# Two products of no use ahead of each transposition, and a transposition whose PSUM banks hold halves of the heads

## The chip, the core and the metric

The kernel runs on one core of a Trainium2 chip. A core has a matrix engine (TensorE, in profiles PE; its weight loads are shown as PEld), VectorE (DVE), ScalarE (ACT), GpSimd (POOL) and SyncE (SP), each with its own in-order queue of instructions; DMA engines move data. They wait for one another by semaphores. TensorE writes to PSUM, in banks, and ScalarE and VectorE read them there. The metric is the device time of one execution in microseconds (us); lower is better.

## What is computed

A block-sparse attention (4 batches, 8 heads, 768 positions, 64 per head, blocks of 32), and behind it a mixing of tokens and channels:

```python
    mask = np.abs(blk_i - blk_j) <= window
    mask = mask | (blk_i == 0) | (blk_j == 0) | (blk_i == n_blocks - 1) | (blk_j == n_blocks - 1)
    for qb in range(n_blocks):
        for kb in sampled_blocks[qb]:
            mask[qb * block:(qb + 1) * block, kb * block:(kb + 1) * block] = True
    ...
    attn = np.exp(scores)
    attn = attn / (np.sum(attn, axis=-1, keepdims=True) + 1e-09)
    return np.matmul(attn, v).astype(np.float32)
...
    theta = x @ w_theta
    ...
    y = yr + yi
    u = x + y
    return (u + np.maximum(u @ w_ch, 0.0)).astype(np.float32)
```

Each block of 32 queries sees its neighbours, the first and last block and three blocks drawn at random; the first and the last block see all. The change concerns the attention alone, in f32.

## The kernel before, in words

The attention is cut into 56 units (lines 441 to 443): for each of two pairs of batches, six *outer* units (marked "w": the first and last query block against a third of all keys each) and 22 *inner* ones, one for each query block between. An inner unit holds one query block of 16 heads: two batches b, four places p (these lie on the partitions, 4 x 32 queries) and two halves e of the heads, against 8 key blocks (256 keys). All units pass these stages:

- `scores` (line 320): TensorE writes S, per (e, b) 128 queries by 256 keys, two banks of PSUM; VectorE reduces it to the extreme m (line 342).
- `weights` (line 352): ScalarE makes P = exp, four instructions, one for each (e, b), in the order e0b0, e0b1, e1b0, e1b1 (line 359).
- `turn` (line 363): TensorE transposes P with the help of the identity, eight times 128x128, into T, two PSUM banks of four each (line 369). Bank 0 holds the first 128 keys of all four (e, b), bank 1 the others. The four transpositions into bank 0 come first. The pool for T has two buffers, both used by each unit, so a unit's bank h is free when `evict` of the unit before has read its bank h.
- `evict` (line 371): ScalarE copies the two banks to pT in SBUF, one instruction each (line 375).
- `values` (line 378): TensorE multiplies pT with the values: `va` holds the first 128 keys' rows (window and edge blocks), `vb` the others (gathered); the sum over both is made in PSUM as X (line 393), 64 records in the profile for an inner unit.
- `finish` (line 404): VectorE divides X by the sum of its weights (lines 400 to 402); `store` writes it out.

The order is written out by hand (`manual_schedule`, line 462). The loop at line 490 puts, for step n, into the queues: the scores of unit n+1, gathering of keys for n+3 (GpSimd), a share of an unrelated job for VectorE and ScalarE (decoding the weights of the token mix, class `Decoder`), `turn` of n, `values` of n-1, `evict` of n, `weights` of n+1, a key copy and the scaling of queries for n+3 on ScalarE, `finish` of n-1, loads for later units. So TensorE's queue runs S(n+1), T(n), X(n-1), S(n+2), T(n+1), ..., and ScalarE's P(n), key copy, scaling, decoding, eviction(n), P(n+1).

Ahead of all units, TensorE makes ten products of the identity with itself that nothing reads (lines 470 to 472). Behind the units, the token mix (from line 548) runs to the end. In the profile, names with `_w` are the outer units': `T_w`, `P_w`.

Of the kernel before, what the change touches and what calls it, by code (L numbers as in the profile page):

```python
# [183 lines left out]
def attention(tc, qT, qE, kT, vr, sampled, xs, ident, early_pieces, late_pieces, first_places, follow, spares):  # L184
# [13 lines left out]
    nc = tc.nc  # L198
    with ExitStack() as ctx, ExitStack() as early:
# [60 lines left out]
        def number_blocks(bp, i):  # L260
            def load(k0, k1, engine):
                _, values = nc.values_load_multi_w_load_instructions(
                    tab.block[0:1, 3 * i + k0 : 3 * i + k1], engines=[engine], min_val=0, max_val=NB - 1,
                    skip_runtime_bounds_check_because="Tables clamps the block numbers",
                )
                return list(values)

            numbers[bp, i] = load(0, 2, mybir.EngineType.Pool) + load(2, 3, mybir.EngineType.Activation)
# [94 lines left out]
        def turn(unit):  # L363

            s = st[unit]
            pt = s.pop("P")
            s["T"] = banks = [ps_t.tile([P, 4, 128], F32, tag="T", name=f"T{name(unit)}_{h}") for h in range(2)]
            for k in range(8):
                nc.tensor.transpose(banks[k // 4][:, k % 4], pt[:, (k // 2) % 2, k % 2, 128 * (k // 4) : 128 * (k // 4) + 128], ident)  # L369

        def evict(unit):
            s = st[unit]
# [5 lines left out]
        def values(unit):  # L378
            bp, i, x = unit
            s = st[unit]  # L380
            s["X"] = ps_x.tile([P, 2, 2, 65], F32, tag="X", name=f"X{name(unit)}")
            if i == "w":
                t, a = x
                parts, width = [(wide[bp][2 * t + c], 128) for c in range(2)], 64
            else:
                parts = [(vas[i % 2], 96 if i == 1 else 128), (vbs[(i + 1) % VB], 96 if i == NB - 2 else 128)]
                a, width = 0, 32
            for b in range(2):
                for e in range(2):
                    for c, (v, rows) in enumerate(parts):  # L390
                        for w_ in range(128 // width):
                            rr, v0 = slice(width * w_, width * w_ + width), 260 * (2 * b + e) + 65 * (2 * a + w_)
                            nc.tensor.matmul(  # L393
                                s["X"][rr, b, e, :], s["T"][0:rows, 4 * c + 2 * e + b, rr], v[0:rows, v0 : v0 + 65], start=c == 0, stop=c == 1,
                            )

        def normalised(label, x, out):
# [48 lines left out]
        def name(unit):  # L446
            bp, i, x = unit
            return f"{bp}_w{x[0]}{x[1]}" if i == "w" else f"{bp}_{i}"
# [13 lines left out]
        with tc.manual_schedule():  # L462
# [27 lines left out]
            for n in range(steps):  # L490
# [16 lines left out]
                if due > 1 and decoder.at % 3:  # L507
                    decoder.on_vector()
                do(n, turn)
                do(n - 1, values)  # L510
                if len(units) - 2 <= n < len(units):
                    next(follow)
# [434 lines left out]
```

## Time and profile before

| | |
|---|---|
| three runs | 593.34, 595.84, 599.29 us (median 595.84) |
| profiled execution, its own time | 595.23 us |
| its span, first to last instruction | 593.5 us |
| mean granted TensorE clock | 0.976 of full speed |
| attention part | up to about 252 us of the span |
| token mix | from there to the end |

The profile is a record of one execution: a page with busy times, groups of instructions by source line and a chain of waits from the last instruction back, and views of single stretches in order of time. In a row of a group, `T<-ident,P 128*128 128x128` is what is written and read (weights 128x128 f32), `x352` the number of records, then busy us and mean ns of one, then the idle us of the engine in front of them and who ended it. An f32 product shows as two records with a weight load each, a transposition as one. In a row of a stretch stand the start in us, the length, the engine, the line and operation, the number merged into the row, and in brackets the idle time ahead and what ended it. "issue" is idle time in which the engine waited for nothing that the profile shows. PEclk is the clock granted to TensorE.

### The profile page before, as it was taken

What the parts mean: (1) busy time and instruction counts of PE and PEld (TensorE: products, weight loads), DVE (VectorE), ACT (ScalarE), POOL (GpSimd) and SP (SyncE); (2) the same over time, 40 slices, a digit from 0 to 9 for tenths busy, and PEclk for the clock granted to TensorE, in tenths of its full rate; (3) what the DMA queues carried; (4) which work ended last, traced back from release to release, by engine and by line L of the source; (5) the groups of instructions that cost most, each with busy time, mean ns of one, the idle gap of its engine ahead of it and who ended that gap; (6) DMA issues with size and microseconds to landing.
All of it is one profiled execution on the core that took longest, in us unless ns stands there. A gap on an engine that the chain in (4) does not pass through costs nothing.

```text
span 593.5 us, 17325 instructions
## 1 busy us (share of the span) xinstructions
PE 547.3 (92%) x7092; PEld 434.5 (73%) x7092; DVE 426.5 (72%) x846; ACT 335.3 (57%) x684; POOL 185.6 (31%) x281
## 2 busy tenths in 40 slices
PE   6997786779988888899999999999999999999997
PEld 4775554556645655688888888888888888888886
DVE  3778998978799989879999995657722659614252
ACT  4798687768967878766474562345530446421220
POOL 1389869922588899520000000000000000000000
PEclk9899989889998989999999999999999999999999
DMA  8979999879987988842333132310202311102002
GB/s 311 351 222 270 263 264 253 251 207 313 273 229 211 260 240 225 227 128 76 85 110 87 36 94 86 104 53 8 83 20 80 99 36 35 36 27 81 1 1 106
DMA packets 53087, 86.67 MB, mean 146 GB/s; under 512 B 5392, under 2 KB 31632, under 8 KB 52624
## 3 DMA queue, kind: packets, MB, share of 16 engines
q1 hardware_dynamic: 43200, 53.28, 29.0%
q0 software_dynamic: 6944, 22.85, 14.3%
q10 hardware_dynamic: 2864, 9.44, 5.2%
q8 instruction: 56, 0.92, 0.7%
q14 instruction: 23, 0.19, 0.1%
HBM read 72.95 MB, written 12.58 MB: 144 GB/s over the span
## 4 chain that ended last, share of the span: by engine, by line
PE 73%; DVE 14%; DMA 6%; issue 3%; ACT 2%; SPq 0%; DVEq 0%; ACTq 0%
PE ya L668 23%; PE yb L668 11%; PE T L369 5%; PE S L339 4%; DVE m L342 4%; PE h L609 4%; PE X L393 4%; PE h L612 4%; PE h L610 4%; PE o L693 3%; PE o L694 3%; PE o L695 2%; PE X_w L393 2%; PE T_w L369 2%; DMA k<-in_kT_dram 2%
## 5 line engine op out<-in xcount | busy, mean ns | idle before, releaser
L359 ACT ACTIVATE P<-S,m 128x256 f32<-128x256 f32 x176 | 70.0, 498 | 15.1 <-DVE m L342 13.9
L369 PE MATMUL T<-ident,P 128*128 128x128 f32 x352 | 61.3, 299 | 16.0 <-ACT P L359 12.6
L369 PEld LDWEIGHTS T<-ident,P 128*128 128x128 f32 x352 | 41.2, 146 | 44.7 <-ACT P L359 35.5
L342 DVE TENSOR_REDUCE m<-S 128x4 f32<-128x1024 f32 x44 | 53.5, 1216 | 9.2 <-PE S L339 7.5
L339 PE MATMUL S<-kg,q 64*32 64x256 f32 x1408 | 54.2, 395 | 5.7 <-issue 5.4
L668 PE MATMUL ya<-w_values,zh 128*128 128x512 f32 x160 | 59.4, 395 | 0.0
L375 ACT COPY pT<-T 128x512 f32<-128x512 f32 x88 | 47.8, 599 | 12.9 <-PE T L369 12.6
L393 PE MATMUL X<-vb,pT 128*32 128x65 f32 (+1 forms) x1408 | 48.2, 227 | 6.9 <-issue 6.9
L393 PE MATMUL X<-va,pT 128*32 128x65 f32 (+1 forms) x1408 | 48.8, 230 | 6.1 <-issue 5.5
L313 POOL DMA_INDIRECT vb<-in_vr_dram,rows x44 | 44.5, 1012 | 19.5 <-PE X_w L393 9.2
L297 POOL COPY kg<-k 128x256 f32<-128x256 f32 (+2 forms) x66 | 37.5, 585 | 33.0 <-DMA k<-in_kT_dram 15.9
L668 PE MATMUL ya<-w_keys,zh 128*128 128x512 f32 x128 | 47.6, 396 | 0.0
L276 POOL COPY kg<-k 128x256 f32 x88 | 46.3, 552 | 0.0
L701 DVE SCALAR_TENSOR_TENSOR of<-o,xT 128x512 f32<-128x512 f32 (+1 forms) x24 | 13.3, 557 | 45.7 <-PE o L695 42.5
L393 PEld LDWEIGHTS X<-va,pT 128*32 128x32 f32 (+1 forms) x1408 | 34.1, 114 | 14.7 <-issue 12.2
L668 PE MATMUL yb<-w_values,zh 128*128 128x256 f32 x160 | 44.6, 278 | 0.0
L393 PEld LDWEIGHTS X<-vb,pT 128*32 128x32 f32 (+1 forms) x1408 | 36.2, 115 | 8.7 <-issue 8.6
L306 POOL COPY va<-va 32x1040 f32<-32x1040 f32 (+1 forms) x28 | 32.5, 1160 | 23.3 <-DMA va<-in_vr_dram 13.6
L609 PE MATMUL h<-w_theta_hi,xh 128*128 128x512 f32 x96 | 38.2, 398 | 0.4 <-ACT xh L598 0.4
L625 DVE SCALAR_TENSOR_TENSOR rr<-t,h 128x512 f32<-128x512 f32 x24 | 16.5, 687 | 29.8 <-ACT t L619 29.8
L610 PE MATMUL h<-w_theta_lo,xh 128*128 128x512 f32 x96 | 37.9, 395 | 0.0
L339 PEld LDWEIGHTS S<-kg,q 64*32 64x32 f32 x1408 | 22.8, 108 | 19.1 <-issue 10.3
(175 smaller groups left out, 1460.0 us busy)
## 6 DMA issues: line engine op xcount, KB each, us to landing
va<-in_vr_dram SPq DMA_DIRECT2D x58, 130.0 KB
q<-in_qT_dram SPq DMA_DIRECT2D x22, 256.0 KB
xs<-xo SPq DMA_DIRECT2D x22, 256.0 KB
xr<-xs SPq DMA_DIRECT2D x22, 256.0 KB
xa<-xs SPq DMA_DIRECT2D x88, 64.0 KB
raw_tok_r<-in_w_tok_r_dram ACTq DMA_DIRECT2D x8, 576.0 KB
out_dram<-of SPq DMA_DIRECT2D x16, 256.0 KB
v<-in_vr_dram SPq DMA_DIRECT2D x6, 520.0 KB
```

The source lines that it names most:

```text
L276: nc.gpsimd.tensor_copy(*sampled_keys(bp, i, k))
L297: nc.gpsimd.tensor_copy(kgs[i % 2][:, s0 : s0 + n], ks[bp][:, b0 : b0 + n])
L313: nc.gpsimd.indirect_dma_start(out=vbs[(i + 1) % VB][rows], out_offset=None, in_=vr, in_offset=bass.IndirectOffsetOnAxis(ap=tab.rows[rows, ...
L339: nc.tensor.matmul(sc[32 * p : 32 * p + 32, e, b, :], q[rows, b, p, :], keys[rows, :, 4 * b + p, :], start=True, stop=True)
L342: nc.vector.tensor_reduce(m.rearrange("r (e b) -> r e b", e=2), sc, axis=AX.X, op=ALU.min)
L359: nc.scalar.activation(pt[:, e, b], sc[:, e, b], AF.Exp, bias=m[:, 2 * e + b : 2 * e + b + 1], scale=-1.0)
L369: nc.tensor.transpose(banks[k // 4][:, k % 4], pt[:, (k // 2) % 2, k % 2, 128 * (k // 4) : 128 * (k // 4) + 128], ident)
L375: nc.scalar.copy(out[:, 4 * h : 4 * h + 4], bank)
L393: nc.tensor.matmul(s["X"][rr, b, e, :], s["T"][0:rows, 4 * c + 2 * e + b, rr], v[0:rows, v0 : v0 + 65], start=c == 0, stop=c == 1,)
L609: nc.tensor.matmul(ps, hi[:, c, :], wh[:, c, :], start=c == 0, stop=False)
L610: nc.tensor.matmul(ps, hi[:, c, :], wl[:, c, :], start=False, stop=False)
L668: nc.tensor.matmul(acc, z[:, dd], wt[:, t0 : t0 + n], start=first and (n == 512 or c % 2 == 0), stop=last, skip_group_check=n == 256,)
```

## The change

Ahead of each inner unit's transposition, TensorE multiplies the identity by itself twice, once into the last quarter of each of the two banks of T, where a transposition afterwards writes over it; no one reads the two products. For inner and outer units alike, bank e now holds the four transposed quarters of head half e (both batches b, both key halves c) where bank c held key half c; the eight transpositions come in the order e, b, c. `values` goes through (e, b) where it went through (b, e), and reads the quarters from their new places. `evict` is the same code.

```diff
             s["T"] = banks = [ps_t.tile([P, 4, 128], F32, tag="T", name=f"T{name(unit)}_{h}") for h in range(2)]
-            for k in range(8):
-                nc.tensor.transpose(banks[k // 4][:, k % 4], pt[:, (k // 2) % 2, k % 2, 128 * (k // 4) : 128 * (k // 4) + 128], ident)
+
+            for h in range(2 if unit[1] != "w" else 0):
+                nc.tensor.matmul(banks[h][:, 3], ident, ident, start=True, stop=True)
+            for e in range(2):
+                for b in range(2):
+                    for c in range(2):
+                        nc.tensor.transpose(banks[e][:, 2 * b + c], pt[:, e, b, 128 * c : 128 * c + 128], ident)
...
-            for b in range(2):
-                for e in range(2):
+            for e in range(2):
+                for b in range(2):
                     for c, (v, rows) in enumerate(parts):
...
-                                s["X"][rr, b, e, :], s["T"][0:rows, 4 * c + 2 * e + b, rr], v[0:rows, v0 : v0 + 65], start=c == 0, stop=c == 1,
+                                s["X"][rr, b, e, :], s["T"][0:rows, 4 * e + 2 * b + c, rr], v[0:rows, v0 : v0 + 65], start=c == 0, stop=c == 1,
```

## The prediction

> **What bounds the kernel now.** I read the page first, then the busy time of the attention part alone, then the groups of instructions, then the chain of waits. The edit touches only the attention part, from about 28 to 252 us; the token mix behind it is left as it is.
>
> ```profile
> span 593.5 us, 17325 instructions
> core 0: us, PE busy (x) PEld busy (x) DVE busy (x) ACT busy (x) POOL busy (x), PEclk, DMA share, GB/s
> 28.00:252.00 224.00, 187.86 (x4916) 128.67 (x4916) 194.97 (x340) 176.99 (x414) 167.52 (x238) 0.95 0.87 247
> ```
>
> No engine fills these 224 us: VectorE is busy for 195 (87%), TensorE for 188 (84%), ScalarE for 177 (79%). The order of work is a ring, so what matters is who waits in each step. TensorE does in step n the scores of unit n+1, the transposition T of unit n and the values X of unit n-1; T needs ScalarE's four exponentials P, and ScalarE's eviction of T stands ahead of its next exponentials.
>
> ```profile
> L369 PE MATMUL T<-ident,P 128*128 128x128 f32 x352 | 61.3, 299 | 16.0 <-ACT P L359 12.6 <-ACT q L246 1.2 <-ACT kg L279 0.5
> L375 ACT COPY pT<-T 128x512 f32<-128x512 f32 x88 | 47.8, 599 | 12.9 <-PE T L369 12.6
> ```
>
> So the ring stalls both ways: TensorE sat idle 16.0 us in front of transpositions, 12.6 of it for P, and ScalarE 12.9 us in front of evictions, 12.6 of it for T. Which of the two holds in a unit is seen from the weight loads of its transposition. Two units side by side, then the first and last of each kind:
>
> ```profile
> 50.04 1.58 ACT L359 ACTIVATE P<-S,m 128x256 f32<-128x256 f32 x4
> 52.12 0.85 PEld L369 LDWEIGHTS T<-ident,P 128*128 128x128 f32 x8 [0.41 <-ACT kg L279]
> 52.81 1.08 ACT L375 COPY pT<-T 128x512 f32<-128x512 f32 x2 [0.89 <-PE T L369]
> ...
> 207.83 1.57 ACT L359 ACTIVATE P<-S,m 128x256 f32<-128x256 f32 x4 [1.41 <-DVE m L342]
> 208.36 0.14 PEld L369 LDWEIGHTS T<-ident,P 128*128 128x128 f32 x1 [1.03 <-ACT P L359]
> 209.45 0.53 PEld L369 LDWEIGHTS T<-ident,P 128*128 128x128 f32 x5 [0.23 <-ACT P L359]
> ...
> 33.03 1.09 PE L369 MATMUL T<-ident,P 128*128 128x128 f32 x8
> 250.47 1.02 PEld L369 LDWEIGHTS T<-ident,P 128*128 128x128 f32 x8
> ...
> 66.25 0.14 PEld L369 LDWEIGHTS T<-ident,P 128*128 128x128 f32 x1 [1.70 <-ACT P L359]
> 244.96 0.14 PEld L369 LDWEIGHTS T<-ident,P 128*128 128x128 f32 x1 [0.71 <-ACT P L359]
> ```
>
> At 52.12 P had long been written (50.04 + 1.58): TensorE comes late, all eight go in a row, and ScalarE waits 0.89 us for them. At 208.36 P is late: the first transposition waits 1.03 us, the next ones go one for each exponential, and the fourth P releases five at once. Of the 44 inner units 26 are of the first kind (33.03 to 250.47), 13 of the second (66.25 to 244.96), and 5 lie between (they start behind the scores but still wait for the last P).
>
> **The price of a product of no use.** Nothing in the inner units is an f32 product of two 128x128 operands. The nearest row is the warm-up of the same two operands, ten products at the start:
>
> ```profile
> L472 PE MATMUL idle<-ident x20: 274/421/583, 1.7 to 5.8; 128*128 128x128 f32 x20
> L369 PE MATMUL T<-ident,P x352: 269/273/477, 33.0 to 251.5; 128*128 128x128 f32 x176
> 33.10 1.02 PE T L369 x8
> ```
>
> Ten products are 20 records, so one product is two. They start 0.216 us apart ((5.8 - 1.7) / 19). But their durations (min 274, median 421) lie as those of T do between its median at full clock (273) and its longest (477): most of the warm-up ran at half clock. Halved, a record is 0.108 us. From the other side, T's records, one weight load and one pass of 128 columns each, go at 1.02 / 8 = 0.128 us. Four records for two products are therefore 0.43 to 0.51 us; 0.86 if the warm-up's pace were that of the full clock. I take 0.51, by the row of the same place in the program. 44 units make 22 us of new TensorE time, some of it in front of the transposition's own work.
>
> **Its wait.** The first product into each bank now carries the wait for unit n-1's eviction of that bank; behind it in TensorE's queue stand T, X and the next scores. That eviction (52.81 + 1.08 = 53.89 in the example) stands before P of the unit on ScalarE, so it is over before P is; I cost this wait at nothing. The cover is P itself.
>
> **A late TensorE pays all.** In the 26 units the products stand between the scores and the transposition, and nothing waits there: T ends 0.51 us later, 1.02 where the clock is halved. The new order gives nothing back: the first bank is still whole after four of eight.
>
> **A late P gains.** In the 13 units the products run in the idle time (1.03 us at 208.36 against 0.51). After the last P only two transpositions are left, not five: 3 x 0.128 = 0.38 us off the end of T, X and the next scores. In the 5 between, the two meet: the later of "scores + 0.51 + 1.02" and "last P + two transpositions" decides; worked out, 0.43, 0.29 and 0.22 later, 0.13 and 0.19 earlier. The 12 outer units only get the order. X's four groups only change places with the same 64 records, and their evictions were made a step before: nothing.
>
> Over all units this would be 26 x 0.51 - 13 x 0.38 + 0.62 = +8.9 us. But only the transpositions on the chain of waits count:
>
> ```profile
> 60.65 1.02 PE T L369 x8
> 156.67 1.03 PE T L369 x8
> 219.01 1.88 PE T L369 x8
> ...
> 77.03 1.04 PE T L369 x5
> 174.58 0.77 PE T L369 x5
> 246.06 0.77 PE T L369 x5
> ...
> 78.07 1.89 PE X L393 x64
> 79.96 1.43 PE S L339 x32
> 55.26 1.67 issue
> 90.52 2.38 issue
> 96.62 1.86 issue
> ```
>
> On it are ten late-TensorE units at full clock (33.10 to 156.67): 10 x 0.51 = 5.1; the one at 219.01 at half clock: 1.0; two of the units between: 0.7. Together +6.8 us. Against this four late-P units (77.03, 174.58, one at 209.46, 246.06): 4 x 0.38 = 1.5; a fifth at half clock 0.8; two units between and one outer: 0.6. Together -2.9 us.
>
> **The clock.** The granted clock halves for whole stretches of 3.41 us, which begin on one grid (77.37, 128.56 and 179.76 lie 15 of them apart), each behind a stretch with little TensorE work:
>
> ```profile
> 43.24:46.65 3.41, 1.82 (x52) 1.00 0.91 220
> 46.65:50.06 3.41, 3.13 (x103) 1.00 0.97 319
> 73.95:77.37 3.42, 2.07 (x38) 1.00 0.92 249
> 77.37:80.78 3.41, 3.41 (x90) 0.50 0.83 218
> 125.15:128.56 3.41, 1.49 (x39) 1.00 0.72 180
> 128.56:131.97 3.41, 2.56 (x16) 0.50 0.41 154
> 176.34:179.76 3.42, 1.04 (x29) 1.00 0.94 220
> 213.89:217.30 3.41, 1.60 (x74) 1.00 0.96 286
> 43.24:46.65 3.41, 1.01 (x6) 1.00 0.91 220
> ```
>
> There are six such half-clock stretches in the part (the last row is the share of T in the first). The products of a unit run as soon as its scores are done, so they fall into the stretch before only at 73.95, where the scores end at 74.7 and TensorE then waits for P. In the others the gap is a wait for a transfer or for instructions that lies ahead of the products in the queue, or holds only T. Saved there: X 1.89 - 1.02, S 1.43 - 1.02, T 1.04 - 0.77, together about 1.5 us. The Trainium skill, "TensorE: Matmul & The Clock Gate", Part 4, says that transposes do not count as activity for the clock as products do; by it the two products would be worth more than their 0.51 us. The rows do not bear it out: of the 1.82 us at 43.24 1.01 are T, which leaves 0.81 of products, and the clock stayed full, while 1.49 us with no T at 125.15 lost it. By that rule the sum would be the clock rival's below; I give it little.
>
> **Instructions.**
>
> ```profile
> q8 instruction: 56, 0.92, 0.7%
> PE 547.3 (92%) x7092; PEld 434.5 (73%) x7092; DVE 426.5 (72%) x846; ACT 335.3 (57%) x684; POOL 185.6 (31%) x281
> ```
>
> 14184 TensorE instructions over 56 packets are 253 each; 44 x 8 = 352 more are 1.4 packets. TensorE's waits called "issue" (1.67 us at 55.26, 2.38 at 90.52, 1.86 at 96.62, some fifteen in all) look like late packets. Up to 1.4 more of them cost 2.4 us; on the other side the products run while such a packet is under way, and about four times 0.5 us of them vanish in the stall that follows (units ahead of rows like those three). I let the two cancel.
>
> **The sum**, against the profiled execution's own 595.2 us: +6.8 - 2.9 - 1.5 = +2.4, so 597.6 us. Its own time is 0.6 us below the median of the runs shown (595.84); I leave that out.
>
> **The rivals.** *TensorE becomes the bound* (slower). Price: every unit whose products aren't hidden pays, on the chain or off it, +8.9 us; with 0.77 us, which is between the two prices, another 26 x 0.26 = 6.8. Place: the scores of unit n+1 end after P of unit n. It decides from the point where this holds for more than some 30 of the 44 units, since the delay of one T then reaches the next scores. Time 604 to 611. For it: 26 units are there already. Against: VectorE's 87%, which leaves slack to TensorE in the chain's long VectorE stretches.
>
> *The clock stays full* (faster). If the products kept all six stretches at full clock, each 1.7 us shorter, that is -10 us in place of -1.5, with +6.8 - 2.9: 589; if the products also vanish in stalls, 584. Against: the rows at 125.15, 176.34 and 213.89, whose gaps they cannot enter.
>
> *All is swallowed.* The delays end in VectorE's queue and in the instruction stalls, the gains too: 595. For it: VectorE's 87%.
>
> **How the numbers follow.** Forecast as summed 0.47; TensorE becomes the bound 0.22; the clock 0.13; swallowed 0.18. Under 1% (6 us) a measurement of this kernel can hardly tell a change: its three runs lie 6 us apart. "Slower by over 1%" is most of the first rival and a tail of the forecast, 0.23; "faster by over 1%" most of the clock's and a little more, 0.13; the rest, 0.64, is within. The range takes in the swallowed case and the low end of the slow rival, and cuts off most of the clock's: 590 to 606. The forecast's own range is 594 to 602.
>
> **What would show it.** Right: TensorE's record count up by 352 in all (176 products, 176 loads); the products' median near 270 ns at a pace of 0.11 to 0.13 us; in the late-P units the last P releases two transpositions, and the chain shows "T x2" where it had "T x5"; ScalarE's wait for T (12.6 us) rises by some 0.5 us for each unit in it, to 15 to 20; TensorE's wait in front of T falls below 16.0, most of it now in front of the products; half-clock stretches five rather than six. Wrong: a span below 590 with no half-clock stretch left (the clock rival), ScalarE's wait for T above 25 (the slow rival), or a product that waits for the eviction.

## The result, and the profile after

The changed kernel takes 603.97 us (median of 4 runs, 601.58 to 608.89) beside 597.57 us of the kernel before in the same comparison: 1.0149 times as long, with a 95% interval of 1.0111 to 1.0188. This ratio and those below leave out executions in the slower state into which any version of this kernel falls now and then, so they are not the quotients of the medians (1.0107 here). The change costs some 6 to 9 us, where the forecast was +2.4. The profiled execution took 604.93 us, with a span of 603.2.

The head of the page of after, the time of its instruction packets, and the attention part in one window (the columns are those of the prediction's row from 28 to 252 us):

```profile
span 603.2 us, 17692 instructions
PE 560.1 (93%) x7268; PEld 453.6 (75%) x7268; DVE 422.9 (70%) x846; ACT 335.8 (56%) x684; POOL 180.3 (30%) x281
q8 instruction: 57, 0.93, 0.7%
core 0: us, PE busy (x) PEld busy (x) DVE busy (x) ACT busy (x) POOL busy (x), PEclk, DMA share, GB/s
28.00:262.00 234.00, 202.01 (x5123) 148.89 (x5119) 192.04 (x342) 178.79 (x417) 162.54 (x238) 0.97 0.83 237
```

TensorE has 176 more records of products (88 products of two records each) and 176 more weight loads, as announced. The loss is in the attention part: the weight loads of its last transposition start at 259.49 us where they started at 250.47, and what follows them is as long as before to within 1 us. VectorE, at 87% the busiest engine there before, is now at 192 / 234 = 82%; TensorE is at 86%.

The costliest groups of the inner units, from the page (busy, mean ns | idle time before them, and what ended it), and the products alone from the groups by shape:

```profile
L374 PE MATMUL T<-ident,P 128*128 128x128 f32 x352 | 50.2, 282 | 2.7 <-issue 1.5
L380 ACT COPY pT<-T 128x512 f32<-128x512 f32 x88 | 47.7, 597 | 26.7 <-PE T L374 26.4
...
L370 PE MATMUL T<-ident 128*128 128x128 f32 x176 | 33.0, 309 | 0.8 <-ACT pT L380 0.8
```

TensorE's idle time in front of the transposition fell from 16.0 us to 2.7, with 0.8 more in front of the products: it hardly waits for P any more. ScalarE's idle time in front of the evictions rose from 12.9 to 26.7. The ring, which stalled both ways, now stalls one way: TensorE is last in most units.

The waits of the two engines (total us, how many, the longest), and the chain of waits of after:

```profile
ACT pT L380 <- PE T L374: 26.4, 21, 4.9
PE X L398 <- issue: 15.9, 9, 3.3
PE S L339 <- issue: 10.6, 7, 2.7
PE T L374 <- ACT P L359: 1.2, 2, 1.0
PE T L370 <- ACT pT L380: 0.8, 3, 0.3
```

```profile
33.58 0.64 PE T L370 x4
34.22 0.87 PE T L374 x8
...
218.85 3.27 issue
252.13 2.11 issue
```

Products and transposition together take 0.64 + 0.87 = 1.51 us on the chain, where the transposition alone took 1.02: 0.49 us a unit, as priced. But the transposition stands on the chain in 29 of the 44 inner units, where it stood in some 20. And TensorE's largest idle time is still "issue", 28.6 us in all, in 18 waits, beside 17.9 in 15 before. In the waits of before these lines read:

```profile
PE X L393 <- issue: 12.5, 11, 2.4
PE S L339 <- issue: 5.4, 4, 2.5
```

So the books of TensorE between the two windows are: some 14 us more busy time (202.0 against 187.9), 11 us more waits called "issue", 11 us less waiting for P, and some 3 us less of other idle time; the window is 10 us longer. Busy time and "issue" together are 230.6 of the 234 us (205.8 of 224 before). In this profile TensorE and the waits for its instructions fill the part. Which of the two costs the time, and how much of it is the new order's, the experiments have to say. One profile's issue total is not enough for that: second profiles of both kernels, further down, show how far it scatters.

### The profile page after: what moved, and what is told of

The parts are those of the page before. It is cut to its first block, busy times and chain, and to the rows that moved or that the text cites. A ratio compares the mean times of both kernels' runs of the same rounds, so it can differ in the third digit from the quotient of the medians.

```text
span 603.2 us, 17692 instructions
## 1 busy us (share of the span) xinstructions
PE 560.1 (93%) x7268; PEld 453.6 (75%) x7268; DVE 422.9 (70%) x846; ACT 335.8 (56%) x684; POOL 180.3 (30%) x281
## 3 DMA queue, kind: packets, MB, share of 16 engines
q1 hardware_dynamic: 43200, 53.28, 28.6%
## 4 chain that ended last, share of the span: by engine, by line
PE 64%; DVE 18%; DMA 7%; ACT 6%; issue 5%; SPq 0%; DVEq 0%; ACTq 0%
PE ya L673 16%; PE yb L673 8%; PE S L339 6%; PE X L398 5%; PE T L374 5%; PE T L370 3%; PE h L614 3%; PE h L615 3%; PE h L617 3%; DVE m L342 2%; PE o L698 2%; PE o L699 2%; PE o L700 2%; DMA vb<-in_vr_dram 2%; DMA k<-in_kT_dram 2%
## 5 line engine op out<-in xcount | busy, mean ns | idle before, releaser
L380 ACT COPY pT<-T 128x512 f32<-128x512 f32 x88 | 47.7, 597 | 26.7 <-PE T L374 26.4
L398 PE MATMUL X<-va,pT 128*32 128x65 f32 (+1 forms) x1408 | 46.8, 226 | 10.4 <-issue 10.4
L374 PE MATMUL T<-ident,P 128*128 128x128 f32 x352 | 50.2, 282 | 2.7 <-issue 1.5
L398 PE MATMUL X<-vb,pT 128*32 128x65 f32 (+1 forms) x1408 | 46.0, 223 | 5.5 <-issue 5.5
L398 PEld LDWEIGHTS X<-va,pT 128*32 128x32 f32 (+1 forms) x1408 | 33.3, 111 | 21.8 <-issue 18.9
L276 POOL COPY kg<-k 128x256 f32 x88 | 42.4, 508 | 0.0
L370 PEld LDWEIGHTS T<-ident 128*128 128x128 f32 x176 | 24.0, 196 | 20.4 <-ACT P L359 9.9
```

The source lines that it names most:

```text
L276: nc.gpsimd.tensor_copy(*sampled_keys(bp, i, k))
L370: nc.tensor.matmul(banks[h][:, 3], ident, ident, start=True, stop=True)
L374: nc.tensor.transpose(banks[e][:, 2 * b + c], pt[:, e, b, 128 * c : 128 * c + 128], ident)
L380: nc.scalar.copy(out[:, 4 * h : 4 * h + 4], bank)
L398: nc.tensor.matmul(s["X"][rr, b, e, :], s["T"][0:rows, 4 * e + 2 * b + c, rr], v[0:rows, v0 : v0 + 65], start=c == 0, stop=c == 1,)
```

## The experiments

The theory after the result: TensorE's instructions come in packets (57 of them here, about 255 TensorE instructions each), and behind the attention part's transfers the packets come late, so that each added instruction costs, whatever its size (theory B in the expectations). The first rival: the time of the products on TensorE costs (theory A). The second: the new order costs, since it makes TensorE's steps more uneven (theory C). Ratios below are to the kernel before, with 95% intervals; in microseconds they are (ratio - 1) x 596.

That the waits called "issue" are late packets, and not hidden waits for data, can be read from the traces of before and after. Each of the 15 and of the 18 waits ends 1.2 to 1.7 us after a packet of 16 KB of the instruction queue has arrived, and the instructions that end them stand multiples of 256 apart in TensorE's stream, to within one.

**The new order without the products** (the change without its two lines of products):

> The change without its two products: new banks and new order alone. Theory A (the products' own TensorE time, 0.49 us in each inner unit, is paid because TensorE is the last to be ready in almost every unit): at or below the kernel before, ratio 0.990 to 1.000, since the last P now leaves two transpositions and not five. Theory B (the 352 added instructions starve TensorE's instruction supply, whose waits called issue rose from about 18 to 28 us): also 0.990 to 1.000, with issue waits of about 18 us. Theory C (the new order itself costs, since the evictions now wait for both head halves in turn): 1.010 to 1.020.

1.0048 [0.9989, 1.0108]. The value lies above the range of theories A and B and below that of C. The interval holds 1, so a loss is not shown; a gain of the 2.9 us that the prediction gave the order (0.9951) is outside it. The waits of its profile:

```profile
ACT pT L378 <- PE T L372: 20.7, 19, 4.9
PE S L339 <- issue: 17.2, 6, 4.9
PE X L396 <- issue: 14.8, 12, 2.4
PE T L372 <- ACT P L359: 2.5, 3, 1.1
```

The wait for P fell without any product (12.6 to 2.5 us), but this is not what the order was to bring, which was a shorter end behind the last P. It fell together with longer waits elsewhere, behind which TensorE comes to T late: the waits for instructions are 32.6 us instead of 17.9. A run of the order with the old banks, below, shows neither of the two.

**The products without the new order:**

```diff
+            for h in range(2 if unit[1] != "w" else 0):
+                nc.tensor.matmul(banks[h][:, 3], ident, ident, start=True, stop=True)
             for k in range(8):
```

> The kernel before with the two products alone, old banks and order. Theories A and B: 1.012 to 1.020, as the whole change or a little more, because the order's small gain is missing. Theory C: 0.995 to 1.005.

1.0045 [1.0002, 1.0088], 2.7 us. That is under the range of theories A and B and within that of C. The 5.3 us that the chain's pieces gave (6.8 - 1.5) lie at the very edge of the interval, which reaches from nothing to 5.2 us; neither part gives the whole 1.0149 by itself.

**The change with tiny products, and with one wide product for two** (the first keeps the instructions and cuts the time, the second keeps the time and halves the instructions):

```diff
-                nc.tensor.matmul(banks[h][:, 3], ident, ident, start=True, stop=True)
+                nc.tensor.matmul(banks[h][0:32, 3, 0:4], ident[:, 0:32], ident[:, 0:4], start=True, stop=True)
```

```diff
-            for h in range(2 if unit[1] != "w" else 0):
-                nc.tensor.matmul(banks[h][:, 3], ident, ident, start=True, stop=True)
+            if unit[1] != "w":
+                nc.tensor.matmul(banks[0][:, 2:4], ident, ident.unsqueeze(1).to_broadcast([P, 2, P]), start=True, stop=True)
```

> The change with its two products shrunk to 32 x 4 outputs: the same 352 added instructions, but well under 0.1 us in place of 0.49 us a unit. Theory A: 0.992 to 1.003, like the order alone. Theory B: 1.010 to 1.018, like the whole change, with issue waits near 28 us. Theory C: 1.010 to 1.020.

> The change with one product of 256 columns in place of two of 128: the same columns to stream (about 0.43 us a unit), half of the added instructions. Theory A: 1.010 to 1.017, close to the whole change. Theory B: about half of the loss, 1.004 to 1.009. Theory C: 1.010 to 1.020.

1.0142 [1.0066, 1.0218] and 1.0147 [1.0072, 1.0221]. The tiny products came out in theory B's range and the wide one in A's. Neither saves anything beside the whole change, but with intervals of 0.75% each way they cannot tell 2.7 us from nothing, so this pair settles nothing. The tiny products were also dearer than expected, 0.22 us a unit on the chain. Small edits drown here; the next ones were made larger.

**The kernel before once more, unchanged**, to see what an edit of nothing shows:

> The kernel before against itself. All theories: 0.995 to 1.005; the width tells what a difference of a few us is worth. Its profile is a second one of the same program: if the waits called issue (17.9 us in the first) come out anywhere between 15 and 35 us, their size in single profiles of the variants tells nothing by itself.

0.9956 [0.9912, 1.0001], and "issue" of 24.3 us in its profile instead of 17.9. Differences below half a per cent are therefore read as nothing, the 2.7 us of the two products among them, and a difference of 6 us in one profile's issue waits too.

**Sixteen small products, and four full ones, ahead of each inner transposition in the old order.** Sixteen are 64 instructions a unit (2816 in all) and about 0.38 us of TensorE (2.7% of the span on its chain, over 44 units); four are 16 a unit (704) and about 1.0 us:

```diff
+            for z in range(2 if unit[1] != "w" else 0):
+                for c in range(4):
+                    for h in range(2):
+                        nc.tensor.matmul(banks[h][32 * c : 32 * c + 32, 3, 2 * z : 2 * z + 2], ident[64 * h : 64 * h + 64, 0:32], ident[64 * h : 64 * h + 64, 0:2], start=True, stop=True)
             for k in range(8):
```

```diff
+            for h in range(4 if unit[1] != "w" else 0):
+                nc.tensor.matmul(banks[h % 2][:, 3], ident, ident, start=True, stop=True)
             for k in range(8):
```

> The kernel before with sixteen products of 64 x 32 by 2 columns in front of each inner transposition, in place of none: 2816 more TensorE instructions in all (11 packets of 16 KB) in about 0.3 to 0.6 us a unit, the time that two full products take with 352. Theory A (time): 1.003 to 1.008, as with two full products. Theory B (instruction supply): eight times the instructions, 1.025 or more, and issue waits far above 30 us.

> The kernel before with four products in front of each inner transposition, about 1.0 us a unit. Theory A: beyond the first 0.5 us hardly anything is left to hide behind, so most of the second 0.5 us in 44 units comes on top: 1.020 to 1.035. Theory B: twice the instructions of two products, about 1.009.

Sixteen: 1.0463 [1.0408, 1.0518], 27.6 us. Four: 1.0157 [1.0105, 1.0209], 9.4 us. The one with less than half the TensorE time costs three times as much. Packets and waits of sixteen:

```profile
q8 instruction: 67, 1.10, 0.8%
...
PE X L397 <- issue: 23.6, 16, 4.0
PE T L371 <- issue: 11.6, 6, 2.6
PE S L339 <- issue: 8.6, 7, 2.7
```

Eleven more packets (67 against 56), 43.8 us of "issue" in these three lines where there were 17.9, and 27.6 us of time: about 2.5 us a packet, near the length of the longest single waits (2.6 to 4.0). Part of it goes through the clock: its granted clock was 0.960 to 0.970 in all six executions, that of the kernel before beside it 0.966 to 0.986. Four full products came out below theory A's range (1.020 to 1.035) and above B's 1.009. At sixteen's price (27.6 / 2816 = 9.8 ns) their 704 instructions would be 6.9 us; that lies within their interval (6.3 to 12.5 us), so that their time costs beyond this is not shown.

**Eight small products** (the same loop with one z: 1408 instructions), for the line between:

> As with sixteen small products, but eight: 1408 added TensorE instructions (5.6 packets), about 0.2 us a unit. Theory B (each packet of instructions costs about one wait of 2.5 us): half of the 27.6 us, 1.020 to 1.026. Theory A (TensorE time): 1.000 to 1.006.

1.0166 [1.011, 1.0222], 9.9 us, with 61 packets; less than half of sixteen's, and between the ranges of B and A. Eight and sixteen small products make 7 and 10 ns an instruction. The two full ones (352 instructions, 2.7 us, 8 ns) lie on the same line, but are too close to nothing to bear it out. Eight small products, a quarter of the TensorE time of four full ones, cost the same 9 to 10 us.

**The new order of the transpositions alone, with the old banks and the old values:**

```diff
-            for k in range(8):
-                nc.tensor.transpose(banks[k // 4][:, k % 4], pt[:, (k // 2) % 2, k % 2, 128 * (k // 4) : 128 * (k // 4) + 128], ident)
+            for e in range(2):
+                for b in range(2):
+                    for c in range(2):
+                        nc.tensor.transpose(banks[c][:, 2 * e + b], pt[:, e, b, 128 * c : 128 * c + 128], ident)
```

> The kernel before with the transpositions in the new order (both key halves of one head half and batch next to each other), but with the old banks: bank 0 is whole only after the seventh, and nothing is written to the values part. The late-P gain is the same as with the new banks. If the new banks cost (the eviction then carries a wait of its own and the values go through the heads the other way round): 0.992 to 1.000 here. If the order of the transpositions itself costs: 1.003 to 1.010, like the order with the new banks.

1.0024 [0.9983, 1.0065], between its two ranges. The first and the last pair of weight loads of a unit with a late P, and the waits:

```profile
70.36 0.20 PEld L371 LDWEIGHTS T<-ident,P 128*128 128x128 f32 x2 [1.56 <-ACT P L359]
71.45 0.20 PEld L371 LDWEIGHTS T<-ident,P 128*128 128x128 f32 x2 [0.17 <-ACT P L359]
...
PE T L371 <- ACT P L359: 12.4, 13, 2.4
PE X L395 <- issue: 13.0, 11, 2.4
PE S L339 <- issue: 5.9, 6, 1.5
```

Here the order does what the prediction wanted of it. In some twenty units the transpositions go in pairs, and the last P releases two (at 71.45) instead of five; by the trace they end 0.49 us behind it instead of 0.82. TensorE waits for P and for instructions as in the kernel before (12.4 and 18.9 us). And still 0.9951 lies outside the interval: the earlier end of T does not reach the end of the kernel. What takes it up is not shown.

**Half of the inner values' products left out, and half of the inner transpositions.** These take away rather than add. The first takes 0.52 us of TensorE and 64 instructions from each inner unit (each product that is left then starts and ends its own sum, a line not shown), the second 0.51 us and only 8 instructions:

```diff
                     for c, (v, rows) in enumerate(parts):
+                        if i != "w" and c != b:
+                            continue
```

```diff
-            for k in range(8):
+            for k in range(8 if unit[1] == "w" else 4):
...
+            if unit[1] != "w":
+                s["T"] = [banks[0], banks[0]]
```

> The kernel before, with half of the values' products left out in the inner units (the first key half for one batch, the second for the other; part of the result is therefore missing): 0.52 us of TensorE time and 64 instructions less in each, 2816 in all. Theory B: 0.955 to 0.980, as long as no other engine takes over, with far smaller waits called issue. Theory A: the same as leaving out half of the transpositions.

> The kernel before, with half of the transpositions left out in the inner units (the first bank is read twice, so part of the result is wrong): also 0.51 us of TensorE time less in each, but only 8 instructions, 352 in all. Theory B: 0.990 to 0.998. Theory A: the same as leaving out half of the values' products, 0.965 to 0.985.

Half the values' products: 0.9939 [0.9905, 0.9973], 3.6 us faster, far less than either theory expected. Half the transpositions: 0.9998 [0.9959, 1.0037], nothing, just above theory B's range. First the waits of the latter, and a window of before and of it:

```profile
PE X L395 <- issue: 18.2, 22, 3.4
PE S L339 <- issue: 12.1, 7, 3.3
PE T L369 <- ACT P L359: 7.0, 5, 3.9
...
28.00:245.00 217.00, 180.97 (x4801) 123.38 (x4797) 190.14 (x327) 171.31 (x402) 163.84 (x233) 0.95 0.88 249
28.00:245.00 217.00, 174.80 (x4684) 111.12 (x4678) 192.97 (x331) 172.70 (x406) 165.08 (x237) 0.93 0.87 250
```

Of 22 us less of TensorE work (44 x 0.51) nothing reaches the end. One part of it ends in waits for instructions, 30.3 us in two lines where it was 17.9 (15.5 in the second profile of before). Another goes to the clock: the granted clock was 0.951 to 0.974 in its twelve executions, beside 0.967 to 0.990 for the kernel before, and TensorE's busy time in the window fell by only 6 us, from 180.97 to 174.80, since scores and values took longer. Either way the pieces of the chain were no price: T stood on it in some 20 units, at half the work for each, and the time did not move. Then waits and window of the former:

```profile
PE T L369 <- ACT P L359: 17.2, 11, 3.8
PE T L369 <- issue: 5.6, 4, 3.1
...
28.00:245.00 217.00, 178.88 (x3479) 111.72 (x3478) 198.95 (x338) 173.51 (x404) 163.01 (x236) 0.89 0.88 251
```

With 2816 instructions fewer the waits for instructions almost vanish (6.6 us in the whole profile), though the transfers are as dense (DMA share 0.88). That it does not gain as much as sixteen small products lose fits VectorE, busy for 198.95 of 217 us (92%), and the clock, 0.89 in this window where it was 0.95; which of the two holds it back is not shown.

**The change once more:**

> The whole change again, on the chip of the other three. Sum of the parts as measured so far (order alone 2.9 us, two products alone 2.8): 1.007 to 1.013. If the two parts are worse together than apart: 1.013 to 1.019.

1.0102 [1.0042, 1.0161], in the range for the sum of the parts. With the first comparison's 1.0149 the loss is 6 to 9 us. Its profile (604.5 us, as long as the first):

```profile
PE 567.4 (94%) x7268; PEld 457.1 (76%) x7268; DVE 427.2 (71%) x846; ACT 335.6 (56%) x684; POOL 178.1 (30%) x281
...
PE X L398 <- issue: 9.7, 22, 1.2
PE S L339 <- issue: 4.6, 4, 2.6
```

"Issue" is 17.0 us in all here, no more than in the kernel before (17.9 and 24.3), where the first profile showed 28.6; only 8.9 us of it stand behind a packet. What has grown instead is TensorE's busy time, 567.4 us over the span beside 547.3 before and 560.1 in the first profile. So this execution of the change is as slow without more waiting for instructions. Time and waits add up to the same: busy and "issue" together are 584.4 us here, 588.7 in the first profile, and 565.2 and 570.5 in the two of before.

**Lighter transfers.** `light` is the kernel before without the loads of the window's values from the third inner unit on and the gathers from the fifth on; the units compute with stale values. `light_sixteen` adds the sixteen small products to it.

```diff
-            for b0, n in runs:
+            for b0, n in runs if i <= 2 else []:
...
+            if i > VB:
+                return
```

> The kernel before with part of its loads left out: no window values from the third inner unit on and no gathered values from the fifth on in each half (old values stay in place, so the result is wrong). Some 25 MB of the 87 are not moved, nearly all in the attention part. If late packets of instructions are late because of the other transfers: waits called issue far under the 18 to 24 us of the kernel before, and the time falls to 0.96 to 0.99. If they are late by themselves: issue waits unchanged.

> The same with sixteen small products in front of each inner transposition. If the transfers make the packets late: the step from the light kernel is 3 to 12 us in place of 27.6, with issue waits under 20 us. If packets are late by themselves: again 20 to 28 us.

`light`: 0.9867 [0.9819, 0.9915], 7.9 us faster than before. Its window and the waits:

```profile
28.00:245.00 217.00, 189.44 (x4945) 129.74 (x4942) 197.78 (x343) 178.07 (x416) 127.67 (x202) 0.95 0.51 157
...
PE S L341 <- issue: 1.0, 2, 0.9
PE X L395 <- issue: 0.6, 2, 0.4
PE X_w L395 <- issue: 1.1, 1, 1.1
PE T L371 <- ACT P L361: 22.6, 14, 4.0
```

The same TensorE instructions, with the DMA engines busy 0.51 of the time rather than 0.87: 2.7 us of waits for instructions. Their lateness does come from the transfers. VectorE is at 91% (197.78 of 217), and TensorE waits for P. `light_sixteen`: 1.0003 [0.9966, 1.0041], so the step from `light` is 0.0136 or 8.1 us, where the same products cost 27.6 us behind the full transfers. Its waits:

```profile
PE T L373 <- issue: 9.1, 6, 3.0
PE X L399 <- issue: 7.5, 13, 1.6
PE S L341 <- issue: 4.8, 5, 2.6
```

The waits for instructions are back (21.4 us in these lines), and part of them ends in the idle time that `light` had in front of T. So eleven more packets are late behind half the transfers too; that they cost less fits a TensorE which has idle time to give.

**The order taken apart further:** only the values in their new sequence, and the new banks and order with the values in the old sequence.

```diff
-            for b in range(2):
-                for e in range(2):
+            for e in range(2):
+                for b in range(2):
                     for c, (v, rows) in enumerate(parts):
```

> The kernel before with only the values' products going through the head halves first, as in the change. If this is what costs in the new order: 1.003 to 1.006. If not: 0.997 to 1.003.

> The change without its products and with the values' products in the old sequence: new banks and transposition order alone. If banks and the transpositions' order cost: 1.003 to 1.008. If the values' sequence does: 0.996 to 1.002.

0.9993 [0.9952, 1.0033] and 1.0007 [0.997, 1.0044]. No part of the order moves the time by what can be measured. The profile of the latter has 32.8 us of waits for instructions, so both builds with the new banks and no products have more of them than the kernel before (17.9 and 24.3) and the new order with the old banks (18.9); why is not shown.

**The order, and the whole change, on the lighter transfers:**

> The light kernel (the same loads left out, so the result is wrong) with the change's banks and order, no products. If instruction waits swallowed the order's gain: 1 to 3 us under the light kernel, which is 9 to 11 us under the kernel before, 0.981 to 0.986. If the order costs by itself: 2 us above the light kernel, 0.989 to 0.993.

> The light kernel with the whole change. If the loss is mostly late instructions: 0 to 2.5 us above the light kernel, 0.986 to 0.991 of the kernel before. If it is TensorE's time: 5 us or more above the light kernel, 0.995 or more.

The order on `light`: 0.9846 [0.9799, 0.9894], 1.3 us under `light` (0.9867), in the range for a gain that waits for instructions had swallowed, but well within the noise. The whole change on `light`: 0.9892 [0.9844, 0.9939]. So the change costs some 0.25% or 1.5 us there, with a zero well inside the intervals, and not 6 to 9 (`light` was timed on another chip than these two, each beside the kernel before). The waits of the whole change on `light`:

```profile
ACT pT L382 <- PE T L376: 8.7, 9, 3.6
PE T L376 <- ACT P L361: 6.3, 5, 2.1
PE S L341 <- issue: 5.1, 5, 3.0
```

The two products are there in full, 44 x 0.49 us of them. TensorE still waits for P in some units, ScalarE waits 8.7 us for T rather than 26.4, and instructions are waited for 5.8 us in all rather than 28.6. This does not tell time from instructions, though: `light` left TensorE 22.6 us of waiting for P, in which 22 us of products find room whatever their instructions cost.

## Why the prediction was wrong

**What held.** The records: 176 and 176. The price of a product: forecast 0.43 to 0.51 us for two, measured 0.49 on the chain; the median 275 ns where about 270 was forecast (the four records take 0.64 us, 0.16 each, and the transpositions behind them 0.87 rather than 1.02, 0.11 each). The wait for the eviction is small: 0.8 us in 3 waits, though a product that waits for it was named as a sign of being wrong. TensorE's wait in front of T below 16.0 us: 2.7, but most of it is not in front of the products (0.8). The sign of the sum, too. And the sign named for the slow rival came: ScalarE's wait for T went above 25 us, to 26.4.

**The step that failed is "only the transpositions on the chain of waits count".** With it the sum let the products be paid in eleven late units and two between, "+6.8", and let the rest hide. In the change the transposition, with the products ahead of it, stands on the chain in 29 inner units (24 in the second profile). TensorE's idle time in front of it is used up: of 16.0 us 2.7 are left. Busy time and waits for instructions together fill 230.6 of 234 us where they filled 205.8 of 224. The chain of one execution was no price the other way round either: half of the transpositions, worth over 5 us by such a sum, gave 0.9998 [0.9959, 1.0037].

**"A late P gains" (-2.9) failed too, and most plainly.** Three builds of the order without the products measured 1.0048, 1.0024 and 1.0007, each with 1 in its interval and 0.9951 outside. Its mechanism is real: with the old banks the last P releases two transpositions in some twenty units. But the earlier end of T brought nothing that can be measured. Nor was the idle time before it all TensorE's to fill: the 1.03 us at 208.36 are idle time of the weight loads, and that of the transpositions behind them was 0.55. In the change itself TensorE is seldom early enough; the trace shows the pairs in some five units (the last pair of one at 196.00), and the chain has no "T x2".

**"Instructions" was put at nothing ("I let the two cancel") without ground.** It saw the late packets and took up to 2.4 us for them, against 2 us of products that vanish in stalls. Behind the heavy transfers the supply of TensorE's instructions is itself close to a limit: 1408 and 2816 instructions of almost no work cost 9.9 and 27.6 us. An estimate from these, 7 to 10 ns for each of 352, is 2.5 to 3.4 us. No run isolates this for the change itself, and its second profile is as slow with "issue" at 17.0 us.

**"The clock" (-1.5)** was too small. Forecast was one of six half-clock stretches saved. Four are left, so two were (granted clock in the last column but two):

```profile
core 0: us, PE busy (x), PEclk, DMA share, GB/s
76.21:79.62 3.41, 2.80 (x77) 0.56 0.72 246
117.17:120.58 3.41, 3.41 (x41) 0.56 0.83 216
223.35:226.80 3.45, 3.45 (x32) 0.51 0.43 125
254.08:257.49 3.41, 3.26 (x33) 0.50 0.51 152
```

The second profiles have three, against eight before. The part is slower in spite of it. The clock rival, and the rule on transposes that the prediction cites from the Trainium skill ("TensorE: Matmul & The Clock Gate", Part 4), would by the prediction's reading have left no stretch with a product ahead of every inner transposition; that did not come, though the stretches became fewer.

**The rivals.** "TensorE becomes the bound" named the number, 604 to 611, and its sign. It was right that TensorE comes last in most units: the transposition is on the chain in 29, about its "some 30". Its price was the products' time in every unit; whether it is that time or their instructions that is paid, the runs do not separate. Its argument against itself, VectorE's 87%, was no protection: the late packets had already used half of the slack that an engine at 84% seems to have (187.9 us busy and 17.9 us without instructions, of 224).

**What stays open.** How the loss of the change divides between the time and the instructions of its products: the tiny products and the wide one came out alike within 0.75%, and the two profiles of the change show the same length once with more waits for instructions and once with more busy time. Whether the parts add up: products 2.7 us and order 0 to 3 are up to 6, the whole is 6 in one comparison and 9 in the other. Either part alone uses up most of the waiting for P (1.9 us are left with the products alone, 2.5 with the order alone), so it is plausible that the second finds none left; no run isolates this. Nothing that was tried beats the kernel before without leaving work out.

## What to carry to other kernels

In a stage with dense transfers, count TensorE's instructions, products and weight loads, as a resource beside its time: waits named "issue" in front of many-instruction groups say that the supply is near its limit. Here 22 us less of transpositions with nearly the same instructions gained nothing, an earlier end of T gained nothing, and about as much less work with 2816 instructions fewer gained 3.6 us. A sum over the pieces of one execution's chain is no price where several engines are within a few per cent of each other; leave half of the disputed work out and time that, and read the granted clock beside it, which fell here when work was taken away. Before a difference between two single profiles is read, profile the unchanged kernel twice: here its waits for instructions were 17.9 and 24.3 us, and those of the change 28.6 and 17.0.

## What the runs showed of the hardware

The lateness of instruction packets is tied to the transfers, and strongly: "issue" of 17.9 to 24.3 us in the kernel before at a DMA share of 0.87, and 2.7 us with the same TensorE instructions at 0.51. The packets themselves are almost nothing among the transfers (57 packets, 0.93 MB, 0.7% of the engines' time); every such wait in the first profiles of before and after ended 1.2 to 1.7 us after one of them had arrived. An added TensorE instruction of almost no work (a product of 2 columns, or its weight load) cost 7 to 10 ns behind the dense transfers, and 8.1 us / 2816 = 2.9 ns behind the light ones. A product of 32 by 4 elements is not free either: two of them, four records, took 0.22 us where two of 128 by 128 took 0.49. Less work on TensorE lowered its granted clock: with half of the transpositions left out it was 0.951 to 0.974, beside 0.967 to 0.990; with the products of the whole change added it was 0.983 to 0.994.
